# Two blocks of 64x64 squares put back to back in a filter-and-MLP kernel

## The chip, the core and the metric

The kernel runs on one core of one Trainium2 chip. The metric is the device time of the whole program in microseconds (us); the kernel before takes 3657.98 us, the median of 3 runs (3653.22 to 3661.79).

## What is computed

Per batch of 3072 tokens with 256 channels the reference filters the sequence in the frequency domain, and then sends each token through two feed-forward networks. Cut to what matters:

```python
X = rfft(x, axis=1);  Y = X * (filt_r + 1j * filt_i);  y = irfft(Y)        # 8 x 3072 x 256
h = y @ w_in                                                               # 256 -> 1024
solu = h * softmax(h);  ln = (solu - mean) / sqrt(var + 1e-6) * g_ln
x2 = ln @ w_out                                                            # 1024 -> 256
h2 = x2 @ w_in2                                                            # 256 -> 2048
out = (h2 * sigmoid(1.702 * h2)) @ w_out2                                  # 2048 -> 256
```

## The kernel before

The Fourier transform of length 3072 is done as 128 x 24: a product over 128 (`step1`, line 508), then 64 small transforms of length 24. Four of these small transforms make a *quad*: its forward product, the multiplication by the filter and its backward product each work on [128, 512] values (two batches of 256 channels; 256 values wide where a group has a single batch). There are `NQ` = 16 quads per group of batches. The groups are batch 0 (an own class, `EarlyFilter`), then batches 1-2, 3-4, 5-6 and 7.

A quad goes through these steps of class `Filter`: `load2` (nine DMAs, seven for a single batch: constants `gt`, filter `fl_sb`, data `bt`); `forward` (four products of a 64x64 square each, on the four quarters of TensorE, two PSUM tiles `f`); `cross` for each half (two VectorE operations that read `f` and write `xs` and `pw`); `swap` (per half four DMAs that exchange blocks of 32 partitions of `xs` into `pw`); `weigh` (a VectorE addition, `pw<-pw`); `inverse` (four squares again, two PSUM tiles); `copy_z` (two ScalarE copies out of PSUM, `z<-f`) and `store_z` (four DMAs). Forward and inverse both take their PSUM tiles from pool `ps_m`, tag `m`, which has two banks and also serves `yt` (line 788), `x2` (the product at line 888, printed x) and `step1`. A float32 product shows as two passes, so a block of four squares is eight matmul records at line 549.

The rest of the work is per pair of 128 tokens, number n from 0 to 95. Class `First` filters back to the time domain (`y`, line 788), makes `h` in PSUM (line 806; pool `ps_h`, tag `h`, two banks that one tile [128, 1024] fills), takes the row maximum (`top`, nmx, line 812), exp (line 818), product and sum (`weigh`, line 831), squares (`square`, line 842: it writes its result over `h`, so it is the last that needs the banks), normalizes (line 851), shuffles through DRAM (`e_d`), transposes (line 868) and projects (line 888). It does this for halves a = 0 and 1 of the pair, so that the two banks of `h` are used twice per pair. Class `Second` does the second network in steps d: `hidden` (line 959, six products), `tanh`, `gate` (line 971, th), `split_hi` (line 977, gh), `split_lo` (line 983, gl) and `output` (line 1000, six products into `o`); `finish` (line 1011, ob) and `store` send out a block of two pairs every second unit with 16 DMAs.

The order is written out by hand: every step gets a time in a plan, `at(t, step)`, the plan is sorted, and each engine issues its instructions in that order (in order within an engine; across engines they wait for each other by semaphores). Time 16.0 is one *unit*, the work of one pair. Tables `FIRST`, `SECOND`, `FILTER` and `DENSE` hold the times within a unit. Batches 1-2 go by `DENSE`, two quads per unit (the *dense* stage); batches 3 to 7 by `FILTER`, one quad per unit (the *sparse* stages). SyncE (SP) issues nearly all DMAs, one after the other.

Of the kernel before, what the change touches and what calls it, by code (L numbers as in the profile page):

```python
# [10 lines left out]
F32 = mybir.dt.float32  # L11
# [12 lines left out]
B, S, D = 8, 3072, 256  # L24
N1, N2 = 128, 24
NSLOT = N1 // 2
NG = NSLOT // 2
NQ = NG // 2
FF1, FF2 = 1024, 2048
NPAIR = S // 256  # L30
P = 128

Q = 32
H, W = 64, 112
# [4 lines left out]


FIRST = {
    "load": -19.32,
    "y": -15.38,
    "y_lo": -15.1,
    "hidden": ((-13.76, -12.01), (-3.47, -3.27)),
    "top": (-10.69, -2.46),
    "exp": (-10.21, -2.25),
    "weigh": (-9.13, -1.01),
    "square": (-7.95, -0.47),
    "norm": (-7.03, 0.53),  # L50
    "shuffle": (-5.35, 2.41),
    "gather": (-3.48, 4.33),
    "turn": (-1.88, 6.4),
    "u_hi": (-1.23, 6.69),
    "u_lo": (2.23, 7.37),
    "project": ((9.55, 9.93), (12.53, 12.54)),
    "x2_add": (10.54, 12.68),
    "x2_hi": 12.69,
    "x2_lo": 13.57,
}  # L60

SECOND = {
    "tanh": 0.71,
    "gate": 2.05,
    "split_hi": 2.43,
    "split_lo": 3.34,
    "output": 5.0,
    "finish": 5.13,
# [2 lines left out]


FILTER = {
    "slots": (-0.05, 3.33, 4.15, 15.38),
    "first": (-11.12, -5.98, -1.77, 0.9),
    "second": {"load2": -4.87, "forward": 3.89, "cross": (4.31, 5.2), "swap": (5.0, 5.69), "weigh": (8.13, 9.15), "inverse": 13.25, "copy_z": (14.01, 14.37), "store_z": 15.5},
}


DENSE = {  # L80
    "start": 16.32,
    "second": ({"load2": -1.69, "forward": 3.62, "cross": (4.0, 4.6), "swap": (4.7, 5.1), "weigh": (7.85, 8.34), "inverse": 9.05, "copy_z": (9.9, 10.2), "store_z": 10.64}, {"load2": 5.18, "forward": 13.0, "cross": (13.3, 13.6), "swap": (13.5, 14.1), "weigh": (16.08, 16.69), "inverse": 18.9, "copy_z": (19.11, 19.41), "store_z": 21.16}),
}

ORDER = [0, 1, 2, 3, 4, 5, 6, 7, 8, 9, 16, 17, 10, 11, 18, 19, 12, 13, 20, 21, 14, 15, 22, 23]
# [143 lines left out]
def fft_filter_solu_gelu(  # L229
# [20 lines left out]
    def ps(name, bufs):  # L250
        return ctx.enter_context(tc.tile_pool(name=name, bufs=bufs, space=PSUM))
# [6 lines left out]
    ps_h = ps("ps_h", 1)  # L258
    ps_m = ps("ps_m", 2)
# [8 lines left out]
    together = [range(1)] + [range(b, min(b + 2, B)) for b in range(1, B, 2)]  # L268
    z_of = {}

    first = cst.tile([N1, 2 * N1 + R], F32, name="first")
# [178 lines left out]
    def at(t, fn, *args):  # L450
        plan.append((t, len(plan), fn, args))

    def in_order(*times):
        assert all(a < b for a, b in zip(times, times[1:])), times
# [17 lines left out]
    class Filter:  # L472
# [67 lines left out]
                fr=[fl[:, h, 0:1].to_broadcast(both) for h in range(2)],  # L540
                fi=[fl[:, h, 1:2].to_broadcast(both) for h in range(2)])

        def squares(self, m, x, rows):

            out = [ps_m.tile([P, self.nb, D], F32, tag="m", name="f2") for _ in range(2)]
            for r in range(2):
                part = slice(r * H, r * H + rows)
                for c in range(2):
                    nc.tensor.matmul(  # L549
                        out[r][c * H:(c + 1) * H], m[part, c * H:(c + 1) * H], x(r, c)[part],  # L550
                        start=True, stop=True, skip_group_check=True)
            return out

        def forward(self, q):
            v = self.t[q]
            v["f"] = self.squares(v["fwd"], lambda h, w: v["bt"][:, w, :self.nb], 2 * N2)

        def cross(self, q, h):
            v = self.t[q]
# [19 lines left out]
        def weigh(self, q, h):  # L579
            v = self.t[q]  # L580
            nc.vector.tensor_tensor(v["pr", h], v["xw", h], v["pr", h], op=ALU.add)

        def inverse(self, q):
            v = self.t[q]
            v["f"] = self.squares(v["inv"], lambda w, h: v["pr", h], H)

        def copy_z(self, q, w):
            v = self.t[q]
# [128 lines left out]
    def plan_transform(f, first):  # L717
        for i in range(f.steps):
            in_order(*first(i))
            for t, step in zip(first(i), (f.load_x, f.split_x, f.step1, f.store_a), strict=True):  # L720
                at(t, step, i)
# [13 lines left out]
            in_order(early(g), second(g)[1])  # L735
            at(early(g), f.load_gt, g)

    def plan_filter(batches, first, second):
        f = Filter(batches)
        plan_transform(f, first)  # L740
        for q in range(NQ):
            v = second(q)
            in_order(v["load2"], v["forward"])
            for k in range(2):
                in_order(
                    v["forward"], *(v[name][k] for name in ("cross", "swap", "weigh")),
                    v["inverse"], v["copy_z"][k], v["store_z"])
            for name in ("load2", "forward", "inverse", "store_z"):
                at(v[name], getattr(f, name), q)
            for name in ("cross", "swap", "weigh", "copy_z"):  # L750
                for k in range(2):
                    at(v[name][k], getattr(f, name), q, k)

    def segments(start, count):

# [13 lines left out]
    class First:  # L769
# [96 lines left out]
        def turn(self, a):  # L866
            self.ut[a] = p1.tile([P, K1, P], F32, tag="ut", name="ut")
            nc.vector.transpose(  # L868
                out=self.ut[a].rearrange("p k (i t) -> p k i t", t=Q),
                in_=self.e.pop(a).rearrange("p (i k f) -> p k i f", i=P // Q, f=Q))  # L870
# [178 lines left out]
    v = EARLY  # L1049
# [13 lines left out]
        at(v["small"][0], load_gain, b)  # L1063
    at(v["small"][1], lambda: dma(out=sgn_sb, in_=sgn))

    def later(start, steps):
        def second(q):
            move = lambda t: [move(x) for x in t] if isinstance(t, tuple) else start + 16.0 * q + t
            return {name: move(t) for name, t in steps.items()}
        return second  # L1070

    def ahead(i):
        (a, b), (c, d) = v["ahead"]
        n = v["between"]
        t = start2 + a + b * i if i < n else end + c + d * (i - n)
        return [t + dt for dt in v["more"]]

    def dense(q):
        n, k = divmod(q, len(DENSE["second"]))
        return later(DENSE["start"] + 16.0 * (n - q), DENSE["second"][k])(q)  # L1080

    plan_filter(together[1], ahead, dense)
    for batches in together[2:]:

        def piece(i):
            return 16.0 * ((batches[0] - 2) * NPAIR - 1 + i // 4) + FILTER["slots"][i % 4]

        start = 16.0 * ((batches[0] - 2) * NPAIR - 1 + len(batches) * N2 // 8)
        plan_filter(
            batches, lambda i: [piece(i - 4) + d for d in FILTER["first"]],  # L1090
            later(start, FILTER["second"]))
    at(v["unit"], load_unit)
    for w in weight_parts():
        i = w.n
        t = v["convert"][i]
        steps = (w.magnitude, w.clamp, w.shift, w.sign, w.exponent, w.lower)
        if w.by_pe:
            steps, offsets = (*steps, w.split_hi, w.total, w.store_lo), v["weight_pe"]
        else:
            steps, offsets = (  # L1100
                *steps, w.add, w.scale_rows, w.split_hi, w.split_lo), v["weight"]
# [53 lines left out]
```

## Time and profile before

| | us |
|---|---|
| median of 3 runs | 3657.98 |
| the profiled execution's own time | 3657.52 |
| its span, first to last instruction | 3655.7 |
| TensorE busy | 3573.1 (98%) |
| VectorE busy | 2562.9 (70%) |
| ScalarE busy | 1884.5 (52%) |
| GpSimd busy | 496.0 (14%) |

Stretches of the span: to about 207 us batch 0 and the weights; 207 to 553 the dense stage; 842 to 1422, 1709 to 2289 and 2466 to 3032 the sparse stages of batches 3-4, 5-6 and 7; between them units that hold `step1` of the next group or no filter work; from 3032 only `First` and `Second`. How to read it: a busy TensorE is not TensorE at its peak, since matmuls overlap (a 128x512 product takes 0.39 us from start to end, but the next one starts 0.23 us after it). So distances from start to start are read here, and in the steady stretches TensorE's next start is what every time comes down to.

### The profile page before, as it was taken

What the parts mean: (1) busy time and instruction counts of PE and PEld (TensorE: products, weight loads), DVE (VectorE), ACT (ScalarE), POOL (GpSimd) and SP (SyncE); (2) the same over time, 40 slices, a digit from 0 to 9 for tenths busy, and PEclk for the clock granted to TensorE, in tenths of its full rate; (3) what the DMA queues carried; (4) which work ended last, traced back from release to release, by engine and by line L of the source; (5) the groups of instructions that cost most, each with busy time, mean ns of one, the idle gap of its engine ahead of it and who ended that gap; (6) DMA issues with size and microseconds to landing.
All of it is one profiled execution on the core that took longest, in us unless ns stands there. A gap on an engine that the chain in (4) does not pass through costs nothing.

```text
span 3655.7 us, 50697 instructions
## 1 busy us (share of the span) xinstructions
PE 3573.1 (98%) x17084; PEld 2847.4 (78%) x17084; DVE 2562.9 (70%) x3836; ACT 1884.5 (52%) x3288; POOL 496.0 (14%) x1060
## 2 busy tenths in 40 slices
PE   6889999999999999999999999999999999999999
PEld 4466668888777778888787877888888888888887
DVE  6766667667777776666777777667667676676665
ACT  4644445555555555555555555555545555555553
POOL 3010002221111111221111111211111111111110
PEclk8999999999999999999999999999999999999999
DMA  9754554334444443443444444433443432222221
GB/s 265 257 153 132 144 143 129 121 116 124 116 127 119 129 122 110 132 129 111 119 127 124 123 122 117 123 103 104 117 111 103 114 102 80 80 78 80 77 81 27
DMA packets 399733, 437.82 MB, mean 120 GB/s; under 512 B 153280, under 2 KB 313280, under 8 KB 399472
## 3 DMA queue, kind: packets, MB, share of 16 engines
q1 hardware_dynamic: 393840, 428.15, 40.5%
q10 hardware_dynamic: 5632, 6.42, 0.6%
q8 instruction: 135, 2.21, 0.3%
q14 instruction: 126, 1.03, 0.1%
HBM read 228.84 MB, written 176.16 MB: 111 GB/s over the span
## 4 chain that ended last, share of the span: by engine, by line
PE 89%; DVE 4%; DMA 3%; issue 2%; SPq 1%; ACT 1%; POOL 1%; DVEq 0%; ACTq 0%; POOLq 0%
PE o L1000 27%; PE h L959 27%; PE x L888 15%; PE h L806 13%; PE f L549 3%; PE yt L788 2%; PE f L466 1%; DMA a_d<-az 1%; DVE ob L1011 0%; DVE e L831 0%; SPq L577 0%; DMA e<-e_d 0%; DMA bt<-a_d 0%; ACT h L842 0%; DMA pw<-xs 0%
## 5 line engine op out<-in xcount | busy, mean ns | idle before, releaser
L959 PE MATMUL h<-x2s,w 128*128 128x512 f32 (+1 forms) x4704 | 1185.6, 388 | 4.1 <-DVE th L971 4.1
L959 PEld LDWEIGHTS h<-x2s,w 128*128 128x128 f32 x4704 | 861.8, 188 | 217.0 <-issue 39.3
L1000 PE MATMUL o<-gh,w 128*128 128x512 f32 (+1 forms) x3136 | 964.4, 389 | 8.1 <-DVE ob L1011 7.4
L977 ACT CAST gh<-th 128x512 fp32r<-128x512 f32 x768 | 476.7, 621 | 661.1 <-DVE th L971 622.8
L1000 PEld LDWEIGHTS o<-gh,w 128*128 128x128 f32 x3136 | 578.0, 188 | 125.5 <-issue 13.1
L1000 PE MATMUL o<-gl,w 128*128 128x512 f32 (+1 forms) x1568 | 608.1, 388 | 2.0 <-DVE gl L983 2.0
L966 ACT ACTIVATE th<-h 128x512 f32<-128x512 f32 x768 | 457.2, 595 | 264.5 <-PE h L959 261.6
L971 DVE SCALAR_TENSOR_TENSOR th<-th,h 128x512 f32<-128x512 f32 x768 | 522.9, 681 | 49.9 <-ACT th L966 49.4
L983 DVE TENSOR_TENSOR gl<-th,gh 128x512 fp32r<-128x512 f32 x768 | 529.1, 689 | 32.3 <-ACT gh L977 32.2
L900 DVE TENSOR_TENSOR x_sum<-x,x_sum 128x256 f32<-128x256 f32 x192 | 81.5, 425 | 664.5 <-ACT x_sum L899 664.5
L888 PE MATMUL x<-u,w_hi 128*128 128x512 f32 x1536 | 384.3, 392 | 7.7 <-ACT z L590 5.6
L1000 PEld LDWEIGHTS o<-gl,w 128*128 128x128 f32 x1568 | 295.4, 188 | 69.0 <-DVE gl L983 9.6
L888 PEld LDWEIGHTS x<-u,w_hi 128*128 128x128 f32 x1536 | 289.2, 189 | 75.6 <-ACT z L590 12.0
L822 POOL TENSOR_SCALAR q<-se 128x1 f32<-128x1 f32 x192 | 43.6, 227 | 2241.2 <-ACT e L818 2240.9
L851 DVE TENSOR_SCALAR e<-e,nmu,rs 128x1024 f32<-128x1024 f32 x192 | 156.2, 813 | 215.5 <-POOL rs L846 211.9
L899 ACT COPY x_sum<-x 128x256 f32<-128x256 f32 x192 | 71.2, 371 | 454.0 <-PE x L888 453.8
L806 PE MATMUL h<-w_hi,xh 128*128 128x512 f32 x768 | 248.7, 405 | 0.0
L868 DVE STREAM_TRANSPOSE ut<-e 128x1024 f32<-128x1024 f32 x192 | 237.9, 1239 | 14.3 <-DMA e<-e_d 13.3
L818 ACT ACTIVATE e<-h,nmx 128x1024 f32<-128x1024 f32 x192 | 214.1, 1115 | 62.0 <-DVE nmx L812 57.5
L812 DVE TENSOR_REDUCE nmx<-h 128x1 f32<-128x1024 f32 x192 | 234.5, 1222 | 15.4 <-PE h L806 15.0
L842 ACT ACTIVATE h<-e,nmu 128x1024 f32<-128x1024 f32 x192 | 215.2, 1121 | 49.5 <-POOL nmu L834 49.4
L806 PE MATMUL h<-w_hi,xl 128*128 128x512 f32 x768 | 238.0, 391 | 1.9 <-DVE xl L797 1.9
(94 smaller groups left out, 3841.4 us busy)
## 6 DMA issues: line engine op xcount, KB each, us to landing
e_d<-e SPq DMA_DIRECT2D x192, 512.0 KB
e<-e_d SPq DMA_DIRECT2D x768, 128.0 KB
zr<-z_d SPq DMA_DIRECT2D x96, 256.0 KB
fl_sb<-in_groups SPq DMA_DIRECT2D x256, 96.0 KB
pw<-xs SPq DMA_DIRECT2D x384, 64.0 KB
out<-ob SPq DMA_DIRECT2D x764, 32.0 KB
xin<-in_x SPq DMA_DIRECT2D x84, 256.0 KB
a_d<-az SPq DMA_DIRECT2D x84, 256.0 KB
```

The source lines that it names most:

```text
L806: nc.tensor.matmul(hs, xx[:, c, a * P:(a + 1) * P], ww[:, c, f * 512:(f + 1) * 512], start=(m == 0 and c == 0), stop=(m == 2 and c == 1))
L812: nc.vector.tensor_reduce(out=nmx, in_=self.h[a], op=ALU.max, axis=AX.X, negate=True)
L818: nc.scalar.activation(out=e, in_=self.h[a], func=AF.Exp, bias=self.v[a], accum_out=se)
L842: nc.scalar.activation(out=self.h.pop(a), in_=e, func=AF.Square, bias=nmu, accum_out=ssq)
L868: nc.vector.transpose(out=self.ut[a].rearrange("p k (i t) -> p k i t", t=Q), in_=self.e.pop(a).rearrange("p (i k f) -> p k i f", i=P // Q, ...
L888: nc.tensor.matmul(self.x2[c][:, :n].rearrange("p i t -> p (i t)"), w2[f][:, kk, c * P:(c + 1) * P], self.u[:, kk, :n].rearrange("p i a t ...
L959: nc.tensor.matmul(self.part(t, j), ww[:, c, f * P:(f + 1) * P], xx[..., c, :], start=(m == 0 and c == 0), stop=(m == 2 and c == 1))
L966: nc.scalar.activation(out=th, in_=self.t[d], func=AF.Tanh, scale=1.702)
L971: nc.vector.scalar_tensor_tensor(out=self.g[d], in0=self.g[d], scalar=1.0, in1=self.t.pop(d), op0=ALU.add, op1=ALU.mult)
L977: nc.scalar.copy(out=gh, in_=self.g[d])
L983: nc.vector.tensor_tensor(gl, th, gh, op=ALU.subtract)
L1000: nc.tensor.matmul(o, ww[:, h, f], self.part(gg, j), start=(f == 0 and m == 0), stop=(f == K2 - 1 and m == 2))
```

## The change

`forward` and `inverse` are replaced by one step, `Filter.turn(q)`: the four squares of quad q-1's backward product, and right behind them the four of quad q's forward product. There are NQ + 1 turns per group; the first has only a forward, the last only a backward part. The forward results no longer lie in pool `ps_m` but in one tile of pool `ps_h`, tag `h`, the two banks that `First` uses for `h`. `plan_filter` gives `load2` and the steps of a quad as distances from its turn. The tables of times are re-set: one turn per unit at 8.5 (`FILTER`), two at 8.33 and 16.22 (`DENSE`); of `FIRST`, `shuffle` and `gather` come earlier and the second projection stands in one piece.

```diff
 FILTER = {
-    "slots": (-0.05, 3.33, 4.15, 15.38),
-    "first": (-11.12, -5.98, -1.77, 0.9),
-    "second": {"load2": -4.87, "forward": 3.89, "cross": (4.31, 5.2), "swap": (5.0, 5.69), "weigh": (8.13, 9.15), "inverse": 13.25, "copy_z": (14.01, 14.37), "store_z": 15.5},
+    "slots": (-0.19, 3.19, 4.01, 12.98),
+    "first": (-7.78, -3.04, 2.27, 4.9),
+    "turn": (8.5,),
+    "steps": ({"load2": -8.34, "cross": (0.3, 1.2), "swap": (2.48, 3.28), "weigh": (3.99, 6.6), "copy_z": (0.1, 0.4), "store_z": 2.9},),
 }
...
-        def squares(self, m, x, rows):
-
-            out = [ps_m.tile([P, self.nb, D], F32, tag="m", name="f2") for _ in range(2)]
+        def squares(self, out, m, x, rows):
+
             for r in range(2):
                 part = slice(r * H, r * H + rows)
                 for c in range(2):
                     nc.tensor.matmul(
                         out[r][c * H:(c + 1) * H], m[part, c * H:(c + 1) * H], x(r, c)[part],
                         start=True, stop=True, skip_group_check=True)
-            return out
-
-        def forward(self, q):
-            v = self.t[q]
-            v["f"] = self.squares(v["fwd"], lambda h, w: v["bt"][:, w, :self.nb], 2 * N2)
+        def turn(self, q):
+            if q:
+                v = self.t[q - 1]
+                v["f"] = [ps_m.tile([P, self.nb, D], F32, tag="m", name="f3") for _ in range(2)]
+                self.squares(v["f"], v["inv"], lambda w, h: v["pr", h], H)
+            if q < NQ:
+                u = self.t[q]
+                f = ps_h.tile([P, 2, 512], F32, tag="h", name="f2")[:, :, :self.nb * D]
+                u["f"] = [f[:, h].rearrange("p (b d) -> p b d", d=D) for h in range(2)]
+                self.squares(u["f"], u["fwd"], lambda h, w: u["bt"][:, w, :self.nb], 2 * N2)
...
-        def inverse(self, q):
-            v = self.t[q]
-            v["f"] = self.squares(v["inv"], lambda w, h: v["pr", h], H)
```

What stands where on TensorE, in a unit of a sparse stage. Before (f<-bt,gt is the forward block, f<-pw,gt the backward block; w is the weights' tile of each line), the forward block:

```order
L1000 MATMUL o<-gl,w_788 128x512
L549 MATMUL f_10112<-bt,gt 64x512 x2
L549 MATMUL f_10113<-bt,gt 64x512 x2
L806 MATMUL h<-w_hi,xh 128x512 x2
L806 MATMUL h<-w_lo,xh 128x512 x2
L806 MATMUL h<-w_hi,xl 128x512 x2
```

and, later in the same unit, the backward block:

```order
L1000 MATMUL o<-gl,w_788 128x512
L549 MATMUL f_10354<-pw,gt 64x512 x2
L549 MATMUL f_10355<-pw,gt 64x512 x2
L959 MATMUL h_10371<-x2s,w_740 128x512 x6
L1000 MATMUL o<-gh,w_788 128x512 x2
```

Now the same unit has one place (the lines below 549 have moved by 13):

```order
L972 MATMUL h_10157<-x2s,w_740 128x512 x6
L549 MATMUL f_10170<-pw,gt 64x512 x2
L549 MATMUL f_10171<-pw,gt 64x512 x2
L549 MATMUL f_10176<-bt,gt 64x512 x4
L1013 MATMUL o<-gh,w_788 128x512 x2
L1013 MATMUL o<-gl,w_788 128x512
L1013 MATMUL o<-gh,w_788 128x512 x2
L1013 MATMUL o<-gl,w_788 128x512
L901 MATMUL x_10204<-u,w_hi 128x512 x8
```

The block comes after the second half of the first `h` (no longer between its halves), with the six products of `output` between it and the projection x.

TensorE in a unit of the dense stage, before: the block in front of the projection.

```order
L1000 MATMUL o<-gl,w_788 128x512
L549 MATMUL f_2564<-pw,gt 64x512 x2
L549 MATMUL f_2565<-pw,gt 64x512 x2
L888 MATMUL x_2570<-u,w_hi 128x512 x8
L888 MATMUL x_2570<-u,w_lo 128x256 x8
```

Now the same place reads:

```order
L549 MATMUL f_2498<-pw,gt 64x512 x2
L549 MATMUL f_2499<-pw,gt 64x512 x2
L549 MATMUL f_2504<-bt,gt 64x512 x4
L1013 MATMUL o<-gh,w_788 128x512 x2
L1013 MATMUL o<-gl,w_788 128x512
L1013 MATMUL o<-gh,w_788 128x512 x2
L1013 MATMUL o<-gl,w_788 128x512
L901 MATMUL x_2544<-u,w_hi 128x512 x8
```

Between the backward squares and the projection, which takes one of their two PSUM banks, there are now the forward squares and six products of `output`.

SyncE's DMAs in the dense stage, in a unit that stores a block of results, before (gt, fl_sb, bt are `load2`, pw<-xs is `swap`, z_d<-z is `store_z`, e_d and e are `shuffle` and `gather`, out<-ob is `store`):

```order
L577 DMA pw<-xs 32x512 x8
L596 DMA z_d_139<-z 48x2x256 x4
L525 DMA gt<-in_dft 128x256
L530 DMA fl_sb<-in_groups 24x1024 x4
L535 DMA bt<-a_d_138 48x2x256 x4
L1024 DMA out<-ob 32x4x64 x16
L858 DMA e_d<-e 128x1024
L596 DMA z_d_139<-z 48x2x256 x4
L864 DMA e<-e_d 32x4x256 x4
```

and now:

```order
L531 DMA fl_sb<-in_groups 24x1024 x4
L536 DMA bt<-a_d_138 48x2x256 x4
L598 DMA z_d_139<-z 48x2x256 x4
L1037 DMA out<-ob 32x4x64 x16
L583 DMA pw<-xs 32x512 x4
L871 DMA e_d<-e 128x1024
L583 DMA pw<-xs 32x512 x4
L598 DMA z_d_139<-z 48x2x256 x4
L877 DMA e<-e_d 32x4x256 x4
```

The swap of the quad that is turned at 8.33 stands behind the 16 DMAs of `store`, and its second half behind a shuffle.

## Rows read from the trace of the kernel before

**Rows 1.** The page: busy time, share of the span, instructions by engine.

```profile
PE 3573.1 (98%) x17084; PEld 2847.4 (78%) x17084; DVE 2562.9 (70%) x3836; ACT 1884.5 (52%) x3288; POOL 496.0 (14%) x1060
```

**Rows 2.** The chain of waits: start us, us, what; the projection, once per unit.

```profile
355.99 3.06 PE x L888 x16
...
398.77 3.07 PE x L888 x16
...
444.43 3.06 PE x L888 x16
...
932.14 2.77 PE x L888 x16
968.36 2.77 PE x L888 x16
...
3116.29 2.77 PE x L888 x16
...
3184.21 2.77 PE x L888 x16
```

**Rows 3.** Who waited for whom on TensorE, 207:553; total us, times, longest.

```profile
PE x L888 <- ACT z L590: 5.6, 8, 0.9
PE f L549 <- ACT z L590: 4.8, 7, 0.7
PE h L959 <- DVE th L971: 4.1, 8, 1.8
```

**Rows 4.** Timeline of TensorE around a backward block: start us, us, what.

```profile
945.05 0.61 PE L1000 MATMUL o<-gh,w 128*128 128x512 f32 x2
945.50 0.39 PE L1000 MATMUL o<-gl,w 128*128 128x512 f32 x1
945.82 1.09 PE L549 MATMUL f<-pw,gt 64*64 64x512 f32 x8
946.84 1.65 PE L959 MATMUL h<-x2s,w 128*128 128x512 f32 x6
948.33 0.62 PE L1000 MATMUL o<-gh,w 128*128 128x512 f32 x2
```

**Rows 5.** Timeline, the same block's second pass alone.

```profile
946.30 0.61 PE L549 MATMUL f<-pw,gt 64*64 64x512 f32 x4
```

**Rows 6.** Timeline of the weight loads of the same block.

```profile
945.82 0.21 PEld L549 LDWEIGHTS f<-pw,gt 64*64 64x64 f32 x8 [0.35 <-issue]
```

**Rows 7.** Timeline of TensorE around a forward block 256 wide.

```profile
2473.03 0.66 PE L549 MATMUL f<-bt,gt 48*64 48x256 f32 x8
2473.62 0.73 PE L806 MATMUL h<-w_hi,xh 128*128 128x512 f32 x2
```

**Rows 8.** Timeline of TensorE, dense stage: two places that wait for z.

```profile
383.34 1.09 PE L549 MATMUL f<-pw,gt 64*64 64x512 f32 x8
385.10 1.56 PE L549 MATMUL f<-bt,gt 48*64 48x512 f32 x8 [0.67 <-ACT z L590]
386.59 0.73 PE L806 MATMUL h<-w_hi,xh 128*128 128x512 f32 x2
...
396.52 1.59 PE L549 MATMUL f<-pw,gt 64*64 64x512 f32 x8
398.77 1.89 PE L888 MATMUL x<-u,w_hi 128*128 128x512 f32 x7 [0.66 <-ACT z L590]
```

**Rows 9.** Windows: length, busy us by engine, granted clock, DMA share, GB/s.

```profile
207.00:553.00 346.00, 318.94 (x1490) 224.96 (x1489) 236.46 (x352) 150.38 (x260) 33.38 (x79) 0.97 0.51 141
337.50:340.90 3.40, 3.40 (x10) 1.97 (x14) 3.31 (x5) 1.12 (x2) 0.00 (x0) 0.51 0.40 139
```

**Rows 10.** Timeline, sparse unit: row maximum of h, squares over h.

```profile
1142.22 1.22 DVE L812 TENSOR_REDUCE nmx<-h 128x1 f32<-128x1024 f32 x1
...
1147.60 1.12 ACT L842 ACTIVATE h<-e,nmu 128x1024 f32<-128x1024 f32 x1 [0.23 <-POOL nmu L834]
```

**Rows 11.** Timeline of SyncE, dense stage: the issues of one block's results.

```profile
443.72 7.54 SPq L1024 DMA_DIRECT2D out<-ob  x16
```

More of the change, by code (lines that the diff above doesn't have):

```diff
@@ L41 @@
 FIRST = {
-    "load": -19.32,
+    "load": -19.41,
     "y": -15.38,
     "y_lo": -15.1,
-    "hidden": ((-13.76, -12.01), (-3.47, -3.27)),
-    "top": (-10.69, -2.46),
+    "hidden": ((-13.93, -12.47), (-3.34, -3.16)),
+    "top": (-11.05, -2.44),
     "exp": (-10.21, -2.25),
-    "weigh": (-9.13, -1.01),
-    "square": (-7.95, -0.47),
+    "weigh": (-9.13, -1.39),
+    "square": (-7.95, -0.89),
     "norm": (-7.03, 0.53),
[L51 to L54, printed above, removed]
+    "shuffle": (-6.66, 1.15),
+    "gather": (-4.89, 2.95),
+    "turn": (-1.88, 6.43),
+    "u_hi": (1.05, 6.69),
     "u_lo": (2.23, 7.37),
-    "project": ((9.55, 9.93), (12.53, 12.54)),
-    "x2_add": (10.54, 12.68),
+    "project": ((9.49, 9.93), (12.53, 12.54)),
+    "x2_add": (10.48, 12.62),
     "x2_hi": 12.69,
-    "x2_lo": 13.57,
+    "x2_lo": 13.08,
 }
@@ L64 @@
     "gate": 2.05,
-    "split_hi": 2.43,
+    "split_hi": 2.59,
     "split_lo": 3.34,
@@ L73 @@
 FILTER = {
-    "slots": (-0.05, 3.33, 4.15, 15.38),
-    "first": (-11.12, -5.98, -1.77, 0.9),
-    "second": {"load2": -4.87, "forward": 3.89, "cross": (4.31, 5.2), "swap": (5.0, 5.69), "weigh": (8.13, 9.15), "inverse": 13.25, "copy_z": (14.01, 14.37), "store_z": 15.5},
+    "slots": (-0.19, 3.19, 4.01, 12.98),
+    "first": (-7.78, -3.04, 2.27, 4.9),
+    "turn": (8.5,),
+    "steps": ({"load2": -8.34, "cross": (0.3, 1.2), "swap": (2.48, 3.28), "weigh": (3.99, 6.6), "copy_z": (0.1, 0.4), "store_z": 2.9},),
 }
 DENSE = {
-    "start": 16.32,
-    "second": ({"load2": -1.69, "forward": 3.62, "cross": (4.0, 4.6), "swap": (4.7, 5.1), "weigh": (7.85, 8.34), "inverse": 9.05, "copy_z": (9.9, 10.2), "store_z": 10.64}, {"load2": 5.18, "forward": 13.0, "cross": (13.3, 13.6), "swap": (13.5, 14.1), "weigh": (16.08, 16.69), "inverse": 18.9, "copy_z": (19.11, 19.41), "store_z": 21.16}),
+    "turn": (8.33, 16.22),
+    "steps": ({"load2": -4.75, "cross": (0.37, 0.38), "swap": (0.7, 1.15), "weigh": (3.94, 4.39), "copy_z": (0.09, 0.07), "store_z": 1.51}, {"load2": -5.0, "cross": (0.6, 0.66), "swap": (1.49, 2.29), "weigh": (4.0, 5.0), "copy_z": (0.45, 0.3), "store_z": 3.96}),
 }
@@ L736, in plan_early, with plan_filter, turn @@
             at(early(g), f.load_gt, g)
-    def plan_filter(batches, first, second):
+    def plan_filter(batches, first, start, where):
         f = Filter(batches)
         plan_transform(f, first)
[L741 to L750, printed above, removed]
-                for k in range(2):
-                    at(v[name][k], getattr(f, name), q, k)
+        def turn(q):
+            n, k = divmod(q, len(where["turn"]))
+            t = start + 16.0 * n + where["turn"][k]
+            move = lambda d: tuple(t + x for x in d) if isinstance(d, tuple) else t + d
+            return t, {name: move(d) for name, d in where["steps"][k].items()}
+        for q in range(NQ + 1):
+            t, v = turn(q)
+            at(t, f.turn, q)
+            if q:
+                for k in range(2):
+                    at(v["copy_z"][k], f.copy_z, q - 1, k)
+                    in_order(t, v["copy_z"][k], v["store_z"])
+                at(v["store_z"], f.store_z, q - 1)
+            if q < NQ:
+                in_order(v["load2"], t)
+                at(v["load2"], f.load2, q)
+                for k in range(2):
+                    in_order(t, v["cross"][k], v["swap"][k], v["weigh"][k], turn(q + 1)[0])
+                    for name in ("cross", "swap", "weigh"):
+                        at(v[name][k], getattr(f, name), q, k)
     def segments(start, count):
@@ L1064, in fft_filter_solu_gelu @@
     at(v["small"][1], lambda: dma(out=sgn_sb, in_=sgn))
[L1066 to L1070, printed above, removed]
     def ahead(i):
@@ L1076, in ahead @@
         return [t + dt for dt in v["more"]]
[L1078 to L1082, printed above, removed]
+    plan_filter(together[1], ahead, 16.0, DENSE)
     for batches in together[2:]:
@@ L1088, in fft_filter_solu_gelu @@
         start = 16.0 * ((batches[0] - 2) * NPAIR - 1 + len(batches) * N2 // 8)
-        plan_filter(
-            batches, lambda i: [piece(i - 4) + d for d in FILTER["first"]],
-            later(start, FILTER["second"]))
+        plan_filter(batches, lambda i: [piece(i - 4) + d for d in FILTER["first"]], start, FILTER)
     at(v["unit"], load_unit)
```

## The prediction

> **What bounds the kernel now.** I read the page first: TensorE is busy 98% of the span, VectorE 70%, ScalarE 52% [rows 1]. An average hides stages, so next the chain of waits, for the distance from one projection to the one of the next unit [rows 2]. Late in the run, where no filter work is left, two units take 3184.21 - 3116.29 = 67.92, so 33.96 us a unit. A sparse unit, with one forward and one backward block, takes 36.22; a dense unit, with two of each, takes 42.78 and 45.66 in turn, 44.22 on average. What does one block cost? On the timeline [rows 4] normal products start 0.23 apart; the block starts 0.32 after the last product (0.09 more than normal), lasts 1.02 to the next start, and the six products behind it take 1.49 instead of 1.37 (0.12 more). That is 1.23 us per block, in which two passes start 0.48 apart [rows 4, 5]. By this a sparse unit should take 33.96 + 2 x 1.23 = 36.4 and takes 36.2: it is filled, and TensorE's starts are the only bound. A dense unit should take 33.96 + 4 x 1.23 = 38.9, and takes 5.3 more. The list of waits for the dense stage says where [rows 3]: the projection waits for z 8 times, the forward block for z 7 times, h of the second network for the gate 8 times. So there are two kinds of time to be had: seams in all stages, waits in the dense one.
>
> **The seam.** Of the 128 blocks, 60 pairs (15 in each of four groups) now stand back to back. A 256-wide block lasts 0.59 from start to start where a 512-wide one lasts 1.02 [rows 4, 7]; the difference is two passes of 256 columns, so a 512-wide pass streams 0.43. Of the 0.48 between passes 0.05 is exchange; from the second pass at 946.30 to the next start is 0.54, so 0.11 is drain. Per pair one entry (0.09), one exit (0.12) and one drain (0.11) go, and one exchange (0.05) comes: 0.27, rounded down to 0.26, whatever the width. Bounds: entry and exit alone (0.21, if the seam still drains), and all that is not streaming in a block (1.23 - 0.86 = 0.37, if the seam costs nothing). In the sparse stages 45 pairs give 45 x 0.26 = 11.7 us (9.5 to 16.7), and nothing else in them should change, if nothing there waits.
>
> On the lower end: the Trainium skill (TensorE: Matmul & The Clock Gate, Part 3, what overlaps and what doesn't) says that a weight load overlaps a matmul in flight only where its rows of the array differ. By that rule forward loads wait for the backward squares, which use the same rows, the pair saves 0.21 and the sum below would be 3 us smaller. The trace speaks against it: all eight loads of a block, those of its second pass on the same rows too, are over 0.21 us after the first start, while the first pass still streams [rows 6, 5].
>
> **The waits of the dense stage.** The forward block goes to the banks of h, so it can no longer wait for z. Today it starts 385.10 - 383.34 = 1.76 after the backward block instead of 1.02, and its halves then follow one by one, 1.49 instead of 1.02 [rows 8]: 1.21, seven times: 8.5 us. The projection starts 398.77 - 396.52 = 2.25 after the backward block instead of 1.02 [rows 8]: 1.23, eight times: 9.8 us. Now the forward squares (1.0) and six products (1.37) lie between, so the copy is done when the projection comes: gone. The waits for the gate (4.1 us) come from a VectorE that does `cross` in front of it; in the new order `cross` follows the normalization and the gate comes first: gone. Together 22.4. The clock: the stage runs at 0.97 on average, which over 346 us is 346 x 0.03 = 10.4 us lost; one spell of 3.4 us at 0.51 is shown [rows 9], when TensorE had been stopping and starting. If its waits shrink, I expect most spells to go: I take two thirds, 6.8 (0 to 10.4). The 15 pairs of this stage give 3.9. Sum 33.1.
>
> **What is added there.** *The banks of h.* The forward squares now wait until `square` has written over h. From the row maximum's start to the end of the squares is 1147.60 + 1.12 - 1142.22 = 6.5 us [rows 10]. In front of the turn at 8.33 or 8.5 TensorE has five groups of six products (5 x 1.37) and the backward squares (1.0): 7.9, so 1.2 us are left over after semaphores. In front of the turn at 16.22 only four groups: 6.5, so nothing is left; I charge 0.4 for each of eight: 3.2 (0 to 12). *SyncE.* In the units that store results the swap of the 8.33 turn stands behind 16 issues of together 7.5 us [rows 11]. My count of issues behind the turn before it (8 swaps, 4 gathers, 9 loads, 4 stores of z and the 16 results, at 0.47 each by the same row 19.3 us, beside the 19 us between two turns, and the swaps cannot start before `cross`) has the swap 3 to 4 us late; `weigh`, which waits for it on VectorE, then holds back the low half gl, the row maximum behind it, and by that the squares and the next forward block. Some 1.2 us in each of four such units: 4.8 (0 to 12). Moved and hidden: the 60 x 2 ScalarE copies and 4 VectorE operations per quad are the same ones as before at other times; in a sparse unit they lie beside both projections and four groups of six products before anything asks for the banks of h again; an uncovered copy would cost the 1.23 that rows 8 show. `shuffle` and `gather` earlier, the two projections' parts in one piece and the loads of the next quad move no work to TensorE; before 207 us I take the order as worth nothing (-3 to +3), since there TensorE waits for loads.
>
> **Sum.** Dense stage: -33.1 + 3.2 + 4.8 = -25.1 (between -40, all 8 x 5.3 us of excess, and 0). Sparse stages -11.7. Together -36.8, from the profiled execution's 3657.5: 3620.7. The median of the runs shown is 0.5 us off that execution, so I forecast **3620 us**.
>
> **Rivals.**
> *A. The dense stage keeps its waits, at other places* (banks of h, late swaps, the block of results that VectorE takes out of `o`): a chain per quad of turn, cross, swap, weigh, next turn has to fit into half a unit, 19 us, on queues that were late already. Then only 60 x 0.26 = 15.6 remain: 3642. For it speaks that the excess of 5.3 us a unit has more places than the two I remove; against it, that those two alone are 2.3 of it and cannot come back in the same form. [...]
> *B. The dense stage loses all its excess*, spells included: 8 x 5.3 = 42, and 15.6 for the seams: 3600.
> *C. Slower: the banks of h become a wait in every turn.* The forward squares stand between two uses of h; if the squares over h come more than 1.2 us later against TensorE than today (their chain passes VectorE and ScalarE twice each and GpSimd once, in order, behind gates and transposes), each of 62 later turns waits for the rest. It takes 37 / 62 = 0.6 us beyond the slack, so 1.8 us late, to be no faster; at 1.0 us beyond it is 3620.5 + 62 = 3682. Against it: `cross`, four VectorE operations that in a sparse unit stand right in front of that chain today, now stands behind it.
> *D. The seam saves nothing, and the chip drains between backward and forward as between any two blocks, while the waits go*: 3620.7 + 15.6 = 3636.
>
> **How the numbers follow.** Forecast 55%, with its own range 3610 to 3634; A 18%, B 12%, C 7%, D 8%. The range for 8 in 10 takes in B's side to 3603 and A's to 3645. A measurement of this kernel tells about 0.2%, 7 us, from no change. Slower by more than that is C (3666 up) and nothing else, 6%; within it the rest of C and the weak end of A, 8%; faster 86%.
>
> **What would show it.** In the trace of the changed kernel: 16 records of line 549 in a row whose passes start 0.48 apart, also across the middle (0.54 or more there: the seam drains); a sparse unit of 35.95 from projection to projection (36.2 or more: C or D); no waits of the projection or of line 549 for z; dense units near 40.8 on average, every second one longer, and a new wait of line 549 for ScalarE's squares over h, under 0.5 us at each turn. I am wrong if the dense units stay above 43, or if line 549 waits for h in the sparse stages.

## The result and the profile after

The changed kernel takes 3613.95 us (median, 3612.44 to 3617.53); the kernel before, run beside it, 3657.47. The ratio is 0.9882 (95% interval 0.9865 to 0.9899): 43.5 us less, where 36.8 was forecast. The profiled execution takes 3612.88 us with a span of 3611.1, 44.6 less than before.

The page of the changed kernel, as in [rows 1]:

```profile
PE 3539.3 (98%) x17084; PEld 2861.3 (79%) x17084; DVE 2597.0 (72%) x3836; ACT 1868.2 (52%) x3288; POOL 466.9 (13%) x1060
```

TensorE is as full as before and issues as many matmuls; what changed is how far apart they start. To split the gain over the stages I take the start of the first product of `yt` of a unit in the timeline (the unit that filters pair n is unit n):

| stretch | before, us | after, us | change |
|---|---|---|---|
| start to unit 3 | 206.9 | 210.5 | +3.6 |
| units 3 to 10, dense | 345.9 | 319.9 | -26.0 |
| units 19 to 33, 43 to 57 and 64 to 78, sparse | 1617.3 | 1599.3 | -18.0 |
| units between (`step1` or no filter work) | 827.0 | 827.9 | +0.9 |
| unit 79 to the end | 658.8 | 653.6 | -5.1 |

The first line is no effect that can be told: in the profiles of the eleven kernels below it lies anywhere from 205.4 to 212.8. The sparse stretches do not hold quite the same blocks as before: the first unit of each now has only a forward block (it is 0.85, 0.86 and 0.69 shorter), and the last backward block stands in a unit behind the stretch. That is 2.4 of the -18.0; the other 15.6 are the 42 pairs that lie in these stretches, 0.37 each.

The chain of waits of the changed kernel (start us, us, what), the projections as in [rows 2]:

```profile
302.25 2.77 PE x L901 x16
...
341.19 2.77 PE x L901 x16
...
384.64 2.79 PE x L901 x16
...
980.16 2.79 PE x L901 x16
...
1016.02 2.79 PE x L901 x16
...
3117.28 2.77 PE x L901 x16
...
3184.71 2.77 PE x L901 x16
```

A sparse unit is now 1016.02 - 980.16 = 35.86 (35.81 and 35.83 to 35.86 in turn over the stage, 35.82 on average) instead of 36.22. A dense one is 38.94 and 43.45 in turn here: every second one is still long, and from unit 4 on they take 40.8 on average. And the units without filter work, which no edit was expected to touch, take (3184.71 - 3117.28) / 2 = 33.72 instead of 33.96.

The new block on TensorE in a sparse unit (timeline; before, [rows 4]):

```profile
976.63 1.09 PE L549 MATMUL f<-pw,gt 64*64 64x512 f32 x8
977.54 1.04 PE L549 MATMUL f<-bt,gt 48*64 48x512 f32 x8
978.51 0.72 PE L1013 MATMUL o<-gh,w 128*128 128x512 f32 x2
```

and the weight loads of the same block (before, [rows 6]):

```profile
976.63 0.21 PEld L549 LDWEIGHTS f<-pw,gt 64*64 64x64 f32 x8 [0.35 <-issue]
977.11 0.15 PEld L549 LDWEIGHTS f<-bt,gt 48*64 48x64 f32 x4 [0.28 <-ACT h L855]
977.54 0.15 PEld L549 LDWEIGHTS f<-bt,gt 48*64 48x64 f32 x4 [0.28 <-issue]
```

The second passes of the two blocks alone:

```profile
977.11 0.61 PE L549 MATMUL f<-pw,gt 64*64 64x512 f32 x4
977.97 0.61 PE L549 MATMUL f<-bt,gt 48*64 48x512 f32 x4
```

The backward squares last 0.91 to the next start, the forward ones 0.97, where an isolated block lasted 1.02. The four passes start 0.48, 0.43 and 0.43 apart, and the next product comes 0.54 after the last of them. The first four forward loads start at 977.11, together with the second backward pass and 0.43 before their own pass, though they use the same rows of the array: the seam does not drain.

Who waited for whom on TensorE in the dense stage (207 to 535 us; total, times, longest), instead of [rows 3]:

```profile
PE f L549 <- DMA bt<-a_d: 10.1, 4, 3.3
PE f L549 <- ACT h L855: 5.7, 5, 3.9
```

No wait for z, for th or for xl is left. In their place the forward squares wait four times for their data, bt; of the waits for h, 3.9 is that of the first turn of all. Behind the dense stage there are three more (530 to 3030 us), each at the first turn of a sparse stage:

```profile
PE f L549 <- ACT h L855: 1.0, 3, 0.5
```

One of the waits for bt on the timeline:

```profile
358.95 1.09 PE L549 MATMUL f<-pw,gt 64*64 64x512 f32 x8
363.31 1.84 PE L549 MATMUL f<-bt,gt 48*64 48x512 f32 x8 [3.27 <-DMA bt<-a_d]
```

and the queue of SyncE ahead of it:

```profile
337.53 7.70 SPq L1037 DMA_DIRECT2D out<-ob  x16
345.33 2.42 SPq L583 DMA_DIRECT2D pw<-xs  x4
...
353.08 2.99 SPq L877 DMA_DIRECT2D e<-e_d  x4
356.11 0.43 SPq L526 DMA_DIRECT2D gt<-in_dft  x1
356.58 1.61 SPq L531 DMA_DIRECT2D fl_sb<-in_groups  x4
358.24 1.76 SPq L536 DMA_DIRECT2D bt<-a_d  x4
```

The loads of bt are issued from 358.24 on; the squares that need them could have started at 359.86. From 337.53 on the queue has hardly a gap, and 7.70 of the 20.7 us from there to 358.24 are the 16 DMAs of results. Behind the last of the four waits, 2.0 us at 528.68, the granted clock stays at 1.00. Behind this one of 3.27 us it is 0.61 for 4.4 us, so for the most part at the lower of its two levels, 1.2 GHz (window: length, busy us by engine, clock, DMA share, GB/s):

```profile
363.50:367.90 4.40, 4.40 (x19) 2.85 (x17) 3.50 (x6) 1.45 (x4) 0.69 (x2) 0.61 0.38 141
```

### The profile page after: what moved, and what is told of

The parts are those of the page before. It is cut to its first block, busy times and chain, and to the rows that moved or that the text cites. A ratio compares the mean times of both kernels' runs of the same rounds, so it can differ in the third digit from the quotient of the medians.

```text
span 3611.1 us, 50621 instructions
## 1 busy us (share of the span) xinstructions
PE 3539.3 (98%) x17084; PEld 2861.3 (79%) x17084; DVE 2597.0 (72%) x3836; ACT 1868.2 (52%) x3288; POOL 466.9 (13%) x1060
## 3 DMA queue, kind: packets, MB, share of 16 engines
q14 instruction: 125, 1.02, 0.1%
## 4 chain that ended last, share of the span: by engine, by line
PE 92%; DMA 3%; DVE 2%; SPq 1%; issue 1%; ACT 1%; POOL 0%; DVEq 0%; POOLq 0%; ACTq 0%
PE o L1013 28%; PE h L972 27%; PE x L901 15%; PE h L819 13%; PE f L549 3%; PE yt L801 2%; PE f L467 1%; DMA bt<-a_d 1%; SPq L877 1%; DMA e<-e_d 1%; PE f L511 0%; DVE e L844 0%; PE f L705 0%; ACT h L855 0%; DMA xin<-in_x 0%
## 5 line engine op out<-in xcount | busy, mean ns | idle before, releaser
L864 DVE TENSOR_SCALAR e<-e,nmu,rs 128x1024 f32<-128x1024 f32 x192 | 171.2, 891 | 166.5 <-POOL rs L859 150.5
L892 DVE TENSOR_TENSOR u<-ut,u 128x1024 fp32r<-128x1024 f32 x192 | 237.9, 1239 | 30.0 <-ACT u L889 29.8
```

Source lines behind the costliest of these rows:

```text
L892: nc.vector.tensor_tensor(self.u[:, :, 1, a], self.ut.pop(a), self.u[:, :, 0, a], op=ALU.subtract)
```

## The experiments

Each time stands beside the kernel before, run on the same chip, whose median was 3656.5 to 3657.4.

**The seam.** *e1_split*: only TensorE's order changes, the backward squares (a step `back` of their own) go in front of the six products of h that stood ahead of the pair.

```diff
+            at(t - 0.6, f.back, q)
             at(t, f.turn, q)
```

> The changed kernel with the backward squares put one group of six products earlier, so that the pair no longer stands back to back; banks, tables and the order on all other engines stay. Theory (the comparison of the two traces): a pair saves 0.36 us against two blocks apart, whatever its width, so 60 pairs give back 60 x 0.36 = 21.5: 3635, and a sparse unit goes from 35.82 to 36.18. Rival 1 (the prediction's price, 0.26, with the rest of the gain of the sparse units from somewhere else in the order): 3629.5, sparse unit 36.08. Rival 2 (by the rule on weight loads on the same rows, 0.21): 3626.5, sparse unit 36.03.

3632.71 us, ratio 0.9934 (0.9917 to 0.9950), 18.8 above the changed kernel. Sparse units take 36.20 (35.33 in the stage of batch 7, 34.96 in the changed kernel). On the timeline both blocks are isolated again, 1.02 each, with entry and exit:

```profile
1016.19 1.09 PE L549 MATMUL f<-pw,gt 64*64 64x512 f32 x8
1017.21 1.65 PE L975 MATMUL h<-x2s,w 128*128 128x512 f32 x6
1018.79 1.09 PE L549 MATMUL f<-bt,gt 48*64 48x512 f32 x8
1019.81 0.73 PE L1016 MATMUL o<-gh,w 128*128 128x512 f32 x2
```

A pair is worth 0.37 to 0.38 in a sparse unit of either width, not 0.26 and not 0.21. It is worth little in the dense stage (1.2 us in all, not 15 x 0.36 = 5.4). There the list of waits (210 to 538 us) has 6.2 us for bt in e1_split, 3.9 less than in the changed kernel, and 8.4 for h, 2.7 more: a part of what the pair saves is waited out again.

*e9_twice*: a third block in the row.

```diff
-                self.squares(u["f"], u["fwd"], lambda h, w: u["bt"][:, w, :self.nb], 2 * N2)
+                for _ in range(2):
+                    self.squares(u["f"], u["fwd"], lambda h, w: u["bt"][:, w, :self.nb], 2 * N2)
```

> The changed kernel with the four forward squares issued twice in a row in every turn (the same products into the same banks again), to measure what a further block costs that stands in a row with others. Theory: only the first pass of a row pays an exchange of 0.05, later passes start 0.43 apart (0.27 for 256 columns): a sparse unit 35.82 + 0.87 = 36.69, one of a single batch 34.96 + 0.54 = 35.50, and 48 x 0.87 + 16 x 0.54 = 50 us in all: 3664. Rival 1 (the prediction's model, 0.05 per pass): 36.78 and 3670. Rival 2 (a block costs what it costs alone, 1.23 and 0.82): 37.05 and 3686.

3649.54 us, 0.9977 (0.9966 to 0.9988): 35.6 more, not 50. In the steady units of two batches the size is as the theory had it (36.65 to 36.70, +0.84 on average), in those of one batch less (35.37, +0.41 where 0.54 was expected). The dense stage pays only 2.6 where 16 x 0.87 = 14 was expected: its waits are 4 us shorter in total, and the granted clock is 0.98 on average instead of 0.97.

```profile
1019.53 1.90 PE L549 MATMUL f<-bt,gt 48*64 48x512 f32 x16
1021.36 0.73 PE L1014 MATMUL o<-gh,w 128*128 128x512 f32 x2
```

The 16 forward records last 1021.36 - 1019.53 = 1.83, the 8 of the changed kernel 0.97: 0.86 for a further block, 0.43 a pass, and half of that at half the width. A further block pays nothing at its ends. Of the prediction's exchange of 0.05 per pass only the first in a row is left.

**The bank.** *e4_bank*: forward results in `ps_m` again, so the copies of z have to be issued between the two halves of the turn.

```diff
-                f = ps_h.tile([P, 2, 512], F32, tag="h", name="f2")[:, :, :self.nb * D]
-                u["f"] = [f[:, h].rearrange("p (b d) -> p b d", d=D) for h in range(2)]
+                if q:
+                    for w in range(2):
+                        self.copy_z(q - 1, w)
+                u["f"] = [ps_m.tile([P, self.nb, D], F32, tag="m", name="f2") for _ in range(2)]
```

> The changed kernel with the forward results in the two banks of ps_m again, as before the change; the backward squares, the two copies of z and the forward squares then have to follow one another in the program. Theory: the bank is what makes the pair possible: each of 60 turns has TensorE wait for both copies (in the kernel before the forward block came 0.74 later and its halves 0.47 apart, 1.21 in all), the seam is lost too (0.36), and the projection behind it waits for the cross products that read the same banks (about 1): 60 x (1.2 to 2.6) = 72 to 156: 3686 to 3770. Rival: the copies and products hide beside TensorE as they do in the other stages and the order alone makes the gain: under 3630.

3682.89 us, 1.0069 (1.0051 to 1.0087), just under the expected range; slower than before the change.

```profile
997.29 1.09 PE L549 MATMUL f<-pw,gt 64*64 64x512 f32 x8
999.05 1.56 PE L549 MATMUL f<-bt,gt 48*64 48x512 f32 x8 [0.67 <-ACT z L594]
1000.54 0.73 PE L1016 MATMUL o<-gh,w 128*128 128x512 f32 x2
```

1.76 and 1.49, to the hundredth the stall of [rows 8], now in every sparse unit of two batches too: 37.19 instead of 35.82. The second wait that I expected, the projection's for the banks, did not come in the sparse stages; the dense stage has it once (0.9 us). With the forward results in ps_m the pair costs more than it saves. The dense stage takes 336.1 us here, beside 345.9 before the change and 319.9 with it: by this run 16 of its 26 us need the banks of h, and 10 come with the new order.

**The slack of the banks of h.** *e6_early*: the turn of the sparse stages one group of six products earlier; the distances of its steps grow by 0.55, so that nothing else moves.

```diff
-    "turn": (8.5,),
+    "turn": (7.95,),
```

> The changed kernel with the turn of the sparse stages one group of six products earlier on TensorE (7.95), all other engines in the same order. Theory: in the sparse stages the forward squares start 0.78 us after the end of the squares over h, and 0.18 is the least seen, so the slack is 0.60 in the stages of two batches and 0.17 in that of one; a group of six products is 1.37, so 30 turns wait 0.77 each and 15 wait 1.2: 41 us more, 3655, sparse units 36.6 and waits of the forward squares for h in each. Rival: the squares over h come earlier too, since what they wait for on VectorE shifts with TensorE, or the time is made good behind the turn: under 3625.

3664.22 us, 1.0017 (1.0008 to 1.0027): 50 above the changed kernel, 9 more than expected.

```profile
1017.27 1.09 PE L549 MATMUL f<-pw,gt 64*64 64x512 f32 x8
1018.94 1.19 PE L549 MATMUL f<-bt,gt 48*64 48x512 f32 x8 [0.58 <-ACT h L855]
```

The forward squares come 1.67 after the backward ones, not 0.91: 0.76 late, as the slack of 0.60 says. After the stop the forward block itself lasts 1.12 instead of 0.97 (the next product starts at 1020.05), so sparse units take 36.72 (0.90 more) and those of batch 7 36.18 (1.22 more). So the mechanism of the prediction's rival C was real, and the table stood 0.60 us on the right side of it in the stages of two batches and 0.17 in that of batch 7, not 1.2.

**The unpredicted gain.** Before, o waits in every second unit without filter work for VectorE to empty it (kernel before, 3040 to 3640 us):

```profile
PE o L1000 <- DVE ob L1011: 3.3, 9, 1.8
```

*e2_gather* puts `shuffle` and `gather` alone into the kernel before at their new times.

```diff
-    "shuffle": (-5.35, 2.41),
-    "gather": (-3.48, 4.33),
+    "shuffle": (-6.66, 1.15),
+    "gather": (-4.89, 2.95),
```

> The kernel before with shuffle and gather alone at the new times (-6.66 and 1.15; -4.89 and 2.95). Theory: the unpredicted 0.26 us per unit after 3032 us comes from this edit alone (the transpose of the first half waits for the gather in the kernel before, all VectorE work behind it comes 0.58 us late against TensorE, and the block of results leaves o 0.18 us after TensorE wants it, in every second unit): units 33.70 from 81 on, no wait of o for ob, and 4 to 5 us less in all: 3653. Rival: it comes from the other moved times (the squares, u_hi behind them): the tail stays at 33.96 and the time within 1 us of 3657.5.

3658.07 us, 1.0002 (0.9992 to 1.0011), the tail (units from 81 on) at 33.95: that theory fell. The next suspect was VectorE's order; the kernel before has (timeline of VectorE):

```profile
3093.52 0.42 DVE L900 TENSOR_TENSOR x_sum<-x,x_sum 128x256 f32<-128x256 f32 x1 [5.87 <-ACT x_sum L899]
3093.86 0.68 DVE L983 TENSOR_TENSOR gl<-th,gh 128x512 fp32r<-128x512 f32 x1
3094.50 1.23 DVE L812 TENSOR_REDUCE nmx<-h 128x1 f32<-128x1024 f32 x1
3095.64 0.68 DVE L909 TENSOR_TENSOR x2s<-x_sum,x2s 128x512 fp32r<-128x512 f32 x1
```

Behind the row maximum stands `x2_lo` (x2s), and all that follows comes 0.6 later against TensorE. *e5_x2lo* moves it alone (the last two lines of the diff), *e10_piece* also puts the second projection in one piece, as the change does (all four):

```diff
-    "hidden": ((-13.76, -12.01), (-3.47, -3.27)),
+    "hidden": ((-13.76, -12.01), (-3.34, -3.16)),
-    "x2_lo": 13.57,
+    "x2_lo": 13.08,
```

> The kernel before with x2_lo alone at the new time (13.08 instead of 13.57), which puts one VectorE subtraction of 0.6 us ahead of the row maximum instead of behind it. Theory: this edit, not shuffle and gather, is the gain of the units without filter work: all that hangs on the row maximum comes 0.6 us earlier against TensorE, VectorE empties o in time, and units from 81 on take 33.70 instead of 33.96; with the last units some 5 us in all: 3651 to 3653. Rival: the moved squares and u_hi do it: the tail stays at 33.96 and the time at 3657.

3680.34 us, 1.0057 (1.0042 to 1.0072): slower by 23, the theory fell again. The row maximum now starts 1.54 us after h is complete (TensorE's next product starts at 3111.59), before it was 0.20 (3094.30):

```profile
3110.81 0.42 DVE L900 TENSOR_TENSOR x_sum<-x,x_sum 128x256 f32<-128x256 f32 x1 [5.87 <-ACT x_sum L899]
3111.92 0.69 DVE L909 TENSOR_TENSOR x2s<-x_sum,x2s 128x512 fp32r<-128x512 f32 x1 [0.69 <-ACT x2s L906]
...
3113.13 1.22 DVE L812 TENSOR_REDUCE nmx<-h 128x1 f32<-128x1024 f32 x1
```

VectorE waits for the sum x_sum, then for ScalarE's x2s, and the row maximum is queued behind both. The sum starts only 0.78 before 3111.59, since the second part of the projection stands behind six products of h.

> The kernel before with two edits of the change and nothing else: x2_lo at 13.08 and the second half of h at -3.34 and -3.16, by which the second projection stands in one piece ahead of it. Theory: x2_lo alone made VectorE wait for a sum that came six products (1.37 us) later than in the changed kernel, and held back the row maximum; with the projection in one piece the sum is there in time, so both edits together give the gain of the units without filter work: from 81 on 33.70 instead of 33.96, 5 us in all over the last 17 units: 3650 to 3653. Rival: the gain needs the other moved steps too (squares, u_hi, gather): tail 33.96 or more, time 3657 or more.

3652.43 us, 0.9987 (0.9978 to 0.9996): as expected, 4.9 less. The tail takes 33.70, the sparse units 36.21 as before, and TensorE waits for ob 1.5 us after 3040 us instead of 3.3.

```profile
3055.49 0.42 DVE L900 TENSOR_TENSOR x_sum<-x,x_sum 128x256 f32<-128x256 f32 x1 [4.51 <-ACT x_sum L899]
3056.61 0.69 DVE L909 TENSOR_TENSOR x2s<-x_sum,x2s 128x512 fp32r<-128x512 f32 x1 [0.69 <-ACT x2s L906]
...
3057.84 1.23 DVE L812 TENSOR_REDUCE nmx<-h 128x1 f32<-128x1024 f32 x1
```

VectorE idles as long in front of x2s, but the sum now starts 2.15 us ahead of TensorE's next product (3057.64), and the row maximum is back at 0.20 behind it. x2_lo alone loses; the projection in one piece without x2_lo was run only in the changed kernel: *e7_x2back* moves `x2_lo` back there.

```diff
-    "x2_lo": 13.08,
+    "x2_lo": 13.57,
```

> The changed kernel with x2_lo alone back at 13.57, behind the row maximum. Theory: the row maximum and all behind it come 0.6 us later against TensorE; in units from 81 on o waits for ob again, 33.95; in the stages of two batches the slack of the forward squares (0.78 - 0.18 = 0.60) is just used up, so sparse units stay within 0.05 of 35.82, while the stage of one batch (slack 0.17) loses 0.43 in each of 15 turns: 5 + 6 + some 4 in the dense stage: 3625 to 3630. Rival: the place of x2_lo has no bearing on the banks of h: 3614 to 3619.

3637.48 us, 0.9945 (0.9930 to 0.9959): 23.5 above the changed kernel, more than all seams, and 7.5 above the expected range. The tail is back at 33.96, so the two edits gain there only together. In the sparse stages of two batches the forward squares wait once; o waits for ob, as in the tail (840 to 2400 us):

```profile
PE o L1013 <- DVE ob L1024: 2.5, 14, 0.2
PE f L549 <- ACT h L855: 0.2, 1, 0.2
```

0.18 each by the list, and 0.5 in the period: units of 35.83 and 36.33 in turn, for the most part. In these stages it is o and not the banks of h that decides. In the stage of batch 7, with its slack of 0.17, the forward squares do wait (2450 to 3020 us), four times and not at each of 15 turns:

```profile
PE f L549 <- ACT h L855: 1.8, 4, 0.5
```

**The queue of SyncE in the dense stage.** *e3_store* issues the 16 DMAs of results of three blocks behind the next quad's loads:

```diff
-        at(end + v["store"], o.store)
+        at(end + v["store"] + (6.74 if 1 <= block[0] <= 6 else 0.0), o.store)
```

> The changed kernel with the 16 DMAs of results of three blocks of the dense stage put 6.74 sixteenths of a unit later on SyncE, behind the loads of the next quad and the first half's gather instead of ahead of the swap. Theory: the waits of the forward squares for bt (3.3, 3.2 and 2.0 us, in every second unit) are the queue's, so they go, with the spells of half clock that two of them end in: the dense stage loses 8.5 to 12 us: 3602 to 3605. Rival 1: SyncE issues 37 of the 38 us of such a unit, so the wait moves to the next swap, or to the loads of the other turn: 3612 to 3616. Rival 2: bt is late because its transfer is slow, not its issue: no change.

3604.71 us, 0.9856 (0.9838 to 0.9874): 9.2 below the changed kernel. Three of the four waits for bt are gone (the one left, of 2.0 us, is in unit 3, with no results ahead of its loads in the queue); two new ones for the squares over h came, of 1.6 and 1.8 us (waits of TensorE, 240 to 520 us):

```profile
PE f L549 <- ACT h L855: 4.4, 5, 1.8
PE f L549 <- DMA bt<-a_d: 2.0, 1, 2.0
```

Two ways on from there. *e8_late* also moves the first turn of a dense unit, right in front of the projection (the distances of its steps are set anew in the same table; cut here):

```diff
-    "turn": (8.33, 16.22),
+    "turn": (9.05, 16.22),
```

> e3_store with the turn at 8.33 of the dense stage one group of six products later (9.05), right in front of the projection; its copies, cross products and swaps follow it as closely as before. Theory: the waits for the squares over h that are left at these turns in e3_store (0.3 to 1.8 us, 4.4 in all) go, and with them the last spell of half clock: 3599 to 3601. Rival: the projection now comes 0.9 us after the backward squares and the copy of z out of its bank takes that long with its semaphores, so it waits for z as it did before the change, 0.2 to 0.7 in each of 8 units, and the swaps are later: 3605 to 3612.

3605.26 us, 0.9851 (0.9836 to 0.9865): no gain, the rival's time. The waits for h go, and these come (240 to 560 us); the larger one is not the rival's wait for z but one for gl, the low half from VectorE:

```profile
PE o L1013 <- DVE gl L996: 5.8, 4, 2.0
PE x L901 <- ACT z L592: 2.2, 4, 1.2
```

*e11_halves* leaves the turn, and issues the 16 DMAs in two parts, one unit apart:

```diff
+            for k, n in enumerate(o.block):
+                at(end + v["store"] + 6.74 + 16.0 * k, o.store, n)
```

> e3_store with the 16 DMAs of results of the same three blocks in two parts of 8, one unit apart. Theory: what is left in e3_store are two waits for the squares over h of 1.6 and 1.8 us, in units in which SyncE is late with the swaps because it has all 16 issues behind it; spread over two units they go: 3600 to 3602. Rival: these waits come from the squares' own chain on VectorE and ScalarE: 3604 to 3606 as e3_store.

3598.12 us, 0.9841 (0.9825 to 0.9857), the fastest version: 15.8 below the changed kernel, 1.9 below the expected range. What is left (240 to 520 us):

```profile
PE f L549 <- DMA bt<-a_d: 2.0, 1, 2.0
PE f L549 <- ACT h L855: 1.0, 3, 0.4
```

Dense units take 38.1 to 39.0 from unit 4 on, and nearly all of the excess that the prediction counted (5.3 a unit) is gone: a unit without filter work and two pairs are 33.70 + 2 x 2.12 = 37.94, with 2.12 = 35.82 - 33.70.

## Why the prediction was right, and where not

*The seam* was right in kind and too small: 0.37 a pair, at the upper bound (0.37) that was given as "all that is not streaming". The term that failed is the exchange: "one exchange (0.05) comes" was charged at the seam, and the one inside the second block was left standing. Neither is paid (passes 0.48, 0.43 and 0.43 apart), which is the missing 0.10, and e9_twice shows the same for further passes in a row. The 45 pairs of the sparse stages gave 16.8 us instead of 11.7. The rule of the Trainium skill (TensorE: Matmul & The Clock Gate, Part 3, what overlaps and what doesn't), by which only loads for other rows overlap, does not hold here: the loads of the forward squares start at 977.11, beside the second backward pass on the same rows and 0.43 ahead of their own.

*The dense stage* came out at -26.0 where -25.1 was forecast, but by other terms, so that this match is in part luck: the clock's 6.8 did not come, the queue cost more than its 4.8, and waits that nobody had named went. The three waits named went entirely, and so did two unnamed ones (o for ob 3.9 and h for xl 1.7 in the same list as [rows 3]). Two more of unit 3 (x for u 2.1, o for gl 1.8) went as well, but the first turn of all now waits 3.9 for h in that unit. The clock, put at 6.8, gave nothing back: the window from 210.5 to 530.4 still has 0.97 [rows 9], since new stops took the place of old ones. The charge for the banks of h (0.4 at each of the turns at 16.22) was at the wrong place: there h is never waited for; it is at the first turn of all (3.9) and at four turns at 8.33 (1.9 together), where 1.2 us were said to be left over. The charge for SyncE (4.8) named the right cause, 16 issues of 7.5 us, and the wrong victim. Not the swap and VectorE's chain behind it were hit first, but the next quad's loads, issued 20 us later in the same queue. (The chain through the swaps is hit in e3_store, by the 1.6 and 1.8 us that go in e11_halves.) Of the 10.1 us, 8.5 at three turns go with e3_store. With e11_halves the stage takes 306.2 instead of 319.9: these 13.7 us, clock included, are the price of the 16 issues' place, above the upper bound of 12. The sign "dense units near 40.8 on average" came true, but it does not follow from the prediction's own sum, which gives 44.22 - 25.1 / 8 = 41.1.

*What was costed at nothing*: that "the two projections' parts in one piece" and the rest of the order move no work to TensorE was true, and it was not free of effect. With x2_lo it saves 4.9 us in the kernel before (e10_piece) and its loss costs 23.5 in the new one (e7_x2back). I had read 33.96 as TensorE's own pace without asking for the waits in that stretch; the list of them had 3.3 us for ob. The rest of the moved steps was not taken apart one by one.

*The rivals.* A's mechanism (a chain too tight on queues that were late) is what the bt waits are, at about half of its price (10.1 of 21; 13.7 by e11_halves). B's 3600 is what the order allows once the queue is mended (3598), in part by gains that B did not have (the seam's 0.37 and the end). C's wait for h came in the sparse stages too, which the prediction had called a sign of being wrong, but only at the first turn of each (1.0 us together) and not at every turn: there the slack was 0.60 us, and 0.17 in the stage of batch 7, where three more units are 0.1 to 0.4 longer. D is refuted by e1_split and by the passes 0.43 apart.

The profiled execution gained 44.6 where 36.8 was forecast. The 7.8 us more are the seam of the sparse stages (16.8 instead of 11.7), the units without filter work from 81 on (5.6, not forecast) and the dense stage (0.9), less a start that is 3.6 later in this profile; all other units together changed by 0.1. Why the start scatters stays open.

## What to carry to other kernels

Price a block of small tiles by its neighbours: what one costs alone (1.23) has a part that is paid per row of blocks (0.37), and putting two in a row is worth that only if neither waits for the other's bank. When an order is re-set, look for the wait that the queue's longest burst causes a whole turn later, not at the instruction behind the burst. And before calling a period the engine's own pace, list the waits in it: one of 0.18 us in every second unit cost 0.5 there.

## What was not expected of the hardware

A wait that the list shows with 0.18 us costs TensorE 0.5 in the period (33.71 and 34.21 in turn in e7_x2back), since the product behind it starts 0.34 late and the next two distances are 0.54 and 0.28 instead of 0.45 and 0.23 (timeline of TensorE from 1008.59). A pass of four 64x64 squares, in a row with others, takes 0.43 us for 512 columns and 0.21 for 256 (e9_twice: 0.86 and 0.41 for two more passes), and the passes of the changed kernel start 0.43 apart also where the weights change from the backward to the forward squares.
